# Attention in both directions and a maxout layer: exponentials without maxima, tested on chip, with a branch to a part that recomputes with maxima

## Chip, cores and metric

The kernel runs on one core of a Trainium2 chip. The metric is the device time of one execution in microseconds (us), as the median of several. The engines are named as in the profile: PE is TensorE's matmul, PEld its weight load, DVE is VectorE, ACT is ScalarE, POOL is GpSimd, SP is SyncE (it only issues transfers and waits). A name with a small q, as SPq, is an engine's queue of instructions that do no arithmetic: transfer issues, waits, drains.

## The reference

The inputs are `x` (8 batches, 8 heads, 512 rows, 64 columns) and `state` (8, 8, 32, 64), and four weight matrices. Per batch and head:

```python
scores = scale * x @ state.T                    # 512 x 32
a = exp(scores - scores.max(-1)); a /= a.sum(-1) + 1e-9
xread = a @ state                               # 512 x 64
scores2 = scale * state @ x.T                   # 32 x 512
a2 = exp(scores2 - scores2.max(-1)); a2 /= a2.sum(-1) + 1e-9
sread = a2 @ x                                  # 32 x 64
```

The 512 + 32 rows of the 8 heads side by side make 544 rows of 512 columns per batch, 4352 in all. Each goes through `h = max(X @ w1, X @ w2, X @ w3)` (512 to 768 columns) and `out = h @ w_out` (768 to 512). The inputs are normal numbers times 0.1.

## The kernel before

**Work per batch `b`.** `x_transpose` turns x (on PE, or by a transposing DMA on SP). `scores` multiplies it by the block-diagonal states `bd` and lets ACT take the exponential straight from the accumulators, into `e[b]`: the kernel subtracts no maximum, which changes nothing as long as the exponentials and their sums stay within the range of the numbers. `softmax` sums over the 32 states (line 183, DVE), takes reciprocals (185, DVE) and multiplies (186, POOL or DVE) into `a[b]`. `a_transpose` turns that. `sread` (line 207) uses the same `e` for the other direction: its matmul has columns of ones beside x, so that sums over the 512 rows come with the product; DVE takes the reciprocal of the sum (221, tile `rd`) and multiplies (223). A transposing DMA on SP, issued later, puts the result into `ats`.

**The maxout.** The reading `a @ state` is not formed: `g_cols` multiplies the states by slices of w1, w2, w3 (matmul in line 239, ACT copy in 245), and `x_maxout(b, m)` multiplies that by the transposed `a`, six matmuls of 512 columns for each of six slices `m` of 128 hidden columns. `s_maxout(m)` does the same for all state rows of the 8 batches at once, twelve matmuls of 256 columns. Both are `maxout` (line 253): matmuls in line 260 into three accumulators, ACT copies the first (264), DVE takes the maximum with the second (267) and with the third (268). `ffn_out` (line 280) does the last product, six matmuls (285) per 128 rows, an ACT copy (292) and an output DMA (296, 301). The very last call splits its copy between ACT (289) and DVE (290), and its output DMA is issued by SP.

**Order.** `tc.manual_schedule()` makes each engine issue its instructions in the order in which the text emits them; the framework adds the semaphores. The text staggers the batches: from `b = 2` on a loop runs `x_maxout(b, m)` for `m` in 0 to 5 and after each the functions in `slots[m]`: the next batch's scores, softmax, transposes and `g_cols`, and `ffn_out` of the batch before. For the last batch, `b = 7`, the slots hold `s_maxout(m)` and, in slots 1, 2, 4 and 5, one `ffn_out`. After the loop come six `ffn_out` calls: two of batch 7, two of the state rows, two of batch 7. The end (line 449 in the profile, where the framework's context closes) waits for all transfers, then brings the engines together.

**Buffers.** Accumulators: four one-bank buffers under the tag `pw`, taken in turn by nearly everything here, and two of two banks under `two`.

Of the kernel before, what the change touches and what calls it, by code (L numbers as in the profile page):

```python
# [8 lines left out]
F32 = mybir.dt.float32  # L9
BF16 = mybir.dt.bfloat16  # L10
AX = mybir.AxisListType
AF = mybir.ActivationFunctionType


@with_exitstack
def kernel(
# [14 lines left out]
    nc = tc.nc  # L31

    B, H, S, D = x.shape
    _, _, Ns, _ = state.shape
# [7 lines left out]
    J = 4  # L42
    HS = H // 2
    NM = d_ff // 128
    XW = H * J * D
    scale = 1.0 / (D ** 0.5)

    const = ctx.enter_context(tc.tile_pool(name="const", bufs=1))
    data = ctx.enter_context(tc.tile_pool(name="data", bufs=1))
    wpool = ctx.enter_context(tc.tile_pool(name="weights", bufs=1))  # L50
    work = ctx.enter_context(tc.tile_pool(name="work", bufs=2))
    pp = ctx.enter_context(tc.tile_pool(name="pp", bufs=2, space=bass.MemoryType.PSUM))
# [28 lines left out]
    ident = const.tile([128, 128], BF16, name="ident")  # L81
# [27 lines left out]
    warm = const.tile([128, 1], F32, name="warm")  # L109
    nc.scalar.activation(out=warm, in_=zero[:, 0:1], func=AF.Exp, scale=1.0)  # L110
    ats = data.tile([128, B, HS, Ns], BF16, name="ats")

    def keep_busy(n):
        p = pp.tile([128, 1024], F32, tag="two", name="idle")
        for _ in range(n):
            nc.tensor.matmul(p[:, 0:512], zero[:, 0:128], zero, start=True, stop=True)
# [21 lines left out]
    xT, e, a, aT, G, ht, osb = {}, {}, {}, {}, {}, {}, {}  # L138

    def new(d, b, shape, name, bufs=2):  # L140
        d[b] = work.tile(shape, BF16, tag=name, bufs=bufs, name=name)

    def x_transpose(b, g, copy):

        if g == 0:
            new(xT, b, [128, H, 2, 128], "xT")
        p = pp.tile([128, HS, 2, 128], BF16, tag="pw", bufs=4, name="pxt")
        for s in range(HS):
            for jj in range(2):
                nc.tensor.transpose(  # L150
                    p[:, s, jj, :],
                    xv[b][:, 2 * s + g, 2 * jj:2 * jj + 2, :].rearrange("p j d -> p (j d)"), ident)
        copy(out=xT[b].rearrange("p (s g) j t -> p g s j t", g=2)[:, g], in_=p)  # L153

    def x_transpose_dma(b):
        new(xT, b, [128, H, 2, 128], "xT")
        nc.sync.dma_start_transpose(out=xT[b].rearrange("p h j t -> p (h j) t"), in_=x_sb[b][:, 0:XW])

    def scores(b, g0, g1):
# [7 lines left out]
        for jj in range(2):  # L167
            for g in range(g0, g1):
                for s in range(HS):
# [5 lines left out]
                        stop=(g == g1 - 1 and s == HS - 1), skip_group_check=True)  # L175
        nc.scalar.activation(out=e[b][:, :, g0:g1], in_=p, func=AF.Exp, scale=scale)  # L176

    def softmax(b, g0, g1, mul):
        n = g1 - g0
        if g0 == 0:  # L180
            new(a, b, [128, J, 2, HS, Ns], "a")
        den = work.tile([128, J, n, HS], F32, tag=f"den{n}", name="den")
        nc.vector.reduce_sum(out=den, in_=e[b][:, :, g0:g1], axis=AX.X)  # L183
        rden = work.tile([128, J, n, HS], F32, tag=f"rden{n}", name="rden")
        nc.vector.reciprocal(out=rden, in_=den)  # L185
        mul(  # L186
            out=a[b][:, :, g0:g1].rearrange("p j g s n -> p j (g s) n"),
            in0=e[b][:, :, g0:g1].rearrange("p j g s n -> p j (g s) n"),
            in1=rden.rearrange("p j g s -> p j (g s)").unsqueeze(3).to_broadcast((128, J, n * HS, Ns)))
# [14 lines left out]

    late = []

    def sread(b):

        p = pp.tile([128, 2, 2, D], F32, tag="pw", bufs=4, name="psr")
        for j in range(J):  # L210
            for g in range(2):
                for s in range(HS):
                    xj = xv[b][:, 2 * s + g, j, :]
                    both = bass.AP(xj.tensor, xj.offset,
                                   (xj.ap[0], (XW - ((2 * s + g) * J + j) * D, 2), (1, D)))
                    nc.tensor.matmul(  # L216
                        p[32 * s:32 * s + 32, g], e[b][:, j, g, s, :], both,
                        start=(j == 0 and g == 0), stop=(j == J - 1), skip_group_check=True,
                        tile_position=(0, 32 * s))
        rd = work.tile([128, 2, 1], F32, tag="rd", name="rd")  # L220
        nc.vector.reciprocal(out=rd, in_=p[:, :, 1, 0:1])
        sr = work.tile([128, 2, D], BF16, tag="sr", bufs=B, name="sr")
        nc.vector.tensor_mul(out=sr, in0=p[:, :, 0, :], in1=rd.to_broadcast((128, 2, D)))
        late.append(lambda: nc.sync.dma_start_transpose(
            out=ats[:, b].rearrange("p s n -> p (s n)"), in_=sr.rearrange("p g d -> p (g d)")))
# [54 lines left out]
    def ffn_out(b, j, split=False):  # L280
        if j == 0:
            osb[b] = work.tile([128, J, d_model], F32, tag="osb", name="osb")
        p = pp.tile([128, d_model], F32, tag="pw", bufs=4, name="po")
        for m in range(NM):
            nc.tensor.matmul(p, ht[b][:, m, j * 128:(j + 1) * 128], wout_sb[:, m, :],  # L285
                             start=(m == 0), stop=(m == NM - 1))
        o = osb[b]
        if split:
            nc.scalar.copy(out=o[:, j, 0:256], in_=p[:, 0:256])
            nc.vector.tensor_copy(out=o[:, j, 256:512], in_=p[:, 256:512])  # L290
        else:
            nc.scalar.copy(out=o[:, j, :], in_=p)  # L292
        if b == "s":
            for k in range(4 * j, 4 * j + 4):
                r0 = k * SP + S
                (nc.sync if k % 4 < 2 else nc.gpsimd).dma_start(
                    out=out[r0:r0 + Ns, :], in_=o[32 * (k % 4):32 * (k % 4) + 32, j, :])
            return
        j0 = j if b == B - 1 and j >= 2 else j - 1
        if j == 1 or j == 3 or j0 == j:  # L300
            (nc.sync if b == B - 1 else nc.gpsimd).dma_start(  # L301
                out=out[b * SP:b * SP + S, :].rearrange("(p j) f -> p j f", j=J)[:, j0:j + 1, :],
                in_=o[:, j0:j + 1, :])


    def late_transposes():
        while late:
            late.pop(0)()

    dve, act, pool = nc.vector.tensor_copy, nc.scalar.copy, nc.gpsimd.tensor_copy  # L310
# [3 lines left out]
    states(0, act)  # L314
    for k in range(1, B // 2):
        nc.vector.memset(bds[k], 0.0)
    keep_busy(4)
    dve(out=x0_sb[0], in_=x0_f)
    x_transpose(0, 0, dve)
# [17 lines left out]
    for k in range(1, B // 2):  # L337
        load_st(k, nc.gpsimd)
    load_x(3)
    sread(0)  # L340
    g_cols(0, (1, 2))
    x_maxout(0, 1)
# [39 lines left out]
    for b in range(2, B):  # L382
        n = b + 1
        slots = [[] for _ in range(NM)]
        if n < B:
            if n == 3:
                slots[0].append(lambda: x_transpose(n, 0, act))
                slots[0].append(lambda: x_transpose(n, 1, dve))
                slots[3].append(lambda: x_transpose_dma(n + 1))
            elif n + 1 < B:  # L390
                slots[0].append(lambda: x_transpose_dma(n + 1))
            at = 1 if n == 3 else 0
            slots[at].append(lambda: scores(n, 0, 2))
            slots[at].append(lambda: softmax(n, 0, 2, nc.gpsimd.tensor_mul))
            slots[2 if n == 3 else 1].append(lambda: g_cols(n, (0, 1)))
            slots[2].append(lambda: a_transpose_dma(n))
            slots[3].append(lambda: sread(n))
            slots[4].append(lambda: g_cols(n, (2, 3)))
            slots[5].append(lambda: g_cols(n, (4, 5)))
            slots[4].append(late_transposes)  # L400
            if n % 2 and n + 1 < B:
                slots[3].append(lambda: states((n + 1) // 2, act))
            for k in ((4, 5) if n == 3 else (n + 2,)):
                if k < B:
                    slots[0].append(lambda k=k: load_x(k))
        else:
            for m in range(NM):
                slots[m].append(lambda m=m: s_maxout(m))
        for m in (1, 2, 3, 4, 5) if len(pending) > 4 else (1, 2, 4, 5):
            if pending:  # L410
                slots[m].append(lambda t=pending.pop(0): ffn_out(*t))
        for m in range(NM):
            x_maxout(b, m)
            for f in slots[m]:
                f()
        pending += [(b, j) for j in range(J)]
    assert pending == [(B - 1, j) for j in range(J)]
    ffn_out(B - 1, 0)
    ffn_out(B - 1, 1)
    ffn_out("s", 0)  # L420
    ffn_out("s", 1)
    ffn_out(B - 1, 2)
    ffn_out(B - 1, 3, split=True)


# [28 lines left out]
```

## Time and profile before

| | |
|---|---|
| runs, us | 166.25, 167.53, 166.08 |
| median of the runs, us | 166.25 |
| span of the profiled execution, first to last instruction, us | 164.5 |
| median minus that span, us | 1.75 |
| granted TensorE clock, share of full speed | 1.000 |
| DMA in all, MB | 20.94 |
| last PE matmul ends, us from the span's start | 160.3 |

For the profiled execution the profile gives the span alone; what lies around it is taken as the fourth row. In the profile's lists of groups, a line reads: line of the kernel, engine, operation, output <- input by the program's names, shapes, count, then busy time and mean ns of one, then idle time of the engine just before and what ended it. In the order of time, a line begins with start and duration in us. Lists of waits name who waited for whom, with total, number of times and the longest. The stages of the loop's last batch run from about 131.5 us to 151 us, and the six closing `ffn_out` calls from there to 160.3 us.

### The profile page before, as it was taken

To read this page: it belongs to the slowest core of one execution; us is meant where nothing else is said; L and a number is where in the kernel's file an instruction comes from. 1 tells how busy PE (TensorE), PEld (TensorE's weight loads), DVE (VectorE), ACT (ScalarE), POOL (GpSimd) and SP (SyncE) were. 2 spreads that over 40 slices of the span, in tenths; PEclk is the share of its full clock that TensorE was granted. 3 is DMA by queue.
4 is the path that set the end of the run, shared out by engine and by line. 5 is a ranking of instruction groups with operands and counts; after the bars stand their busy time and mean duration, and the time that the engine had idled before them with its cause. 6 is when DMAs were issued, how large, how long until landed. Compare 5 with 4: busy or idle time off the path is not lost.

```text
span 164.5 us, 3569 instructions
## 1 busy us (share of the span) xinstructions
PE 149.7 (91%) x1432; PEld 70.9 (43%) x1449; DVE 96.0 (58%) x162; ACT 99.1 (60%) x158; POOL 44.0 (27%) x64
## 2 busy tenths in 40 slices
PE   7658699988999999999999999999999999999990
PEld 2425243533445444434344434444444466665430
DVE  4675777889418553665548464865586455585001
ACT  3355578366896678853876688648755853333440
POOL 8975550106150601081016101410141010100140
PEclk9999999999999999999999999999999999999999
DMA  4999999800039999269992989460306030030373
GB/s 132 195 174 199 204 200 248 122 7 0 0 120 130 144 256 198 53 116 145 277 193 87 133 187 104 162 191 14 128 0 195 8 130 0 0 132 0 128 235 148
DMA packets 31824, 20.94 MB, mean 127 GB/s; under 512 B 17184, under 2 KB 29344, under 8 KB 31808
## 3 DMA queue, kind: packets, MB, share of 16 engines
q0 software_dynamic: 15632, 15.08, 46.3%
q1 hardware_dynamic: 16176, 5.64, 18.5%
q8 instruction: 11, 0.18, 0.5%
q14 instruction: 5, 0.04, 0.1%
HBM read 15.20 MB, written 8.91 MB: 147 GB/s over the span
## 4 chain that ended last, share of the span: by engine, by line
PE 63%; DVE 11%; ACT 10%; DMA 6%; POOL 4%; issue 4%; DVEq 0%; ACTq 0%; POOLq 0%
PE pw L260 34%; PE po L285 20%; DMA x<-in_x_dram 4%; PE pg L239 4%; DVE den L183 4%; DVE t L267 3%; ACT e L176 3%; ACT G L245 3%; DVE ht L268 3%; PE ps L171 2%; ACT t L264 2%; PE psr L216 2%; POOL w L94 1%; DMA out_dram<-osb 1%; POOL a L186 1%
## 5 line engine op out<-in xcount | busy, mean ns | idle before, releaser
L260 PE MATMUL pw<-aT,G 128*128 128x512 bf16 x288 | 71.2, 379 | 3.6 <-ACT G L245 1.8
L267 DVE TENSOR_TENSOR t<-t,pw 128x512 bf16<-128x512 bf16 (+1 forms) x54 | 35.1, 650 | 41.6 <-ACT t L264 40.0
L285 PE MATMUL po<-wout,ht 128*128 128x512 bf16 x188 | 47.9, 380 | 0.8
L260 PEld LDWEIGHTS <-G 128*128 128x128 bf16 x288 | 26.7, 98 | 36.2 <-issue 5.1
L245 ACT CAST G<-pg 128x768 bf16<-128x768 f32 x48 | 36.5, 805 | 8.0 <-PE pg L239 7.6
L264 ACT CAST t<-pw 128x512 bf16<-128x512 f32 (+1 forms) x54 | 30.5, 566 | 14.1 <-PE pw L260 12.6
L268 DVE TENSOR_TENSOR ht<-t,pw 128x512 bf16<-128x512 bf16 (+1 forms) x54 | 35.5, 658 | 5.6
L292 ACT COPY osb<-po 128x512 f32<-128x512 f32 x33 | 19.4, 587 | 21.2 <-PE po L285 20.7
L285 PEld LDWEIGHTS <-ht 128*128 128x128 bf16 x204 | 18.4, 98 | 23.6 <-issue 4.7
L301 POOL DMA_DIRECT2D out_dram<-osb x14 | 7.8, 559 | 70.2 <-ACT osb L292 70.2
L186 POOL TENSOR_TENSOR a<-e,rden 128x1024 bf16<-128x1024 bf16 (+1 forms) x8 | 14.4, 1800 | 33.4 <-DVE rden L185 19.8
L239 PE MATMUL pg<-w,bd 64*32 64x384 bf16 x384 | 13.0, 328 | 1.1 <-DMA w<-in_moe_w_dram 1.1
L183 DVE TENSOR_REDUCE den<-e 128x32 f32<-128x1024 bf16 (+1 forms) x9 | 9.9, 1095 | 2.6 <-ACT e L176 2.6
L176 ACT ACTIVATE e<-ps 128x1024 bf16<-128x1024 f32 x7 | 7.2, 1024 | 5.8 <-PE ps L171 5.8
L260 PE MATMUL pw<-ats,w 128*128 128x256 bf16 x72 | 8.8, 273 | 0.0
L239 PEld LDWEIGHTS <-bd 64*32 64x32 bf16 x384 | 3.6, 89 | 11.7 <-issue 11.7
L260 PEld LDWEIGHTS <-w 128*128 128x128 bf16 x72 | 7.0, 98 | 2.1
L94 POOL DMA_DIRECT2D w<-in_moe_w_dram x9 | 6.8, 770 | 0.0
L69 POOL DMA_DIRECT2D x<-in_x_dram x7 | 6.7, 957 | 0.0
L150 PE MATMUL pxt<-ident,x 128*128 128x128 bf16 x64 | 4.4, 219 | 2.2 <-DMA x<-in_x_dram 1.1
L134 ACT COPY bd<-pt 64x512 bf16<-64x512 bf16 x6 | 3.5, 580 | 4.2 <-PE pt L131 4.1
L171 PEld LDWEIGHTS <-xT 128*128 128x128 bf16 x128 | 4.7, 98 | 2.4 <-DVE xT L153 0.8
(42 smaller groups left out, 63.4 us busy)
## 6 DMA issues: line engine op xcount, KB each, us to landing
out_dram<-osb POOLq DMA_DIRECT2D x14, 512.0 KB, 3.7
x<-in_x_dram POOLq DMA_DIRECT2D x7, 512.0 KB, 9.0
w<-in_moe_w_dram POOLq DMA_DIRECT2D x3, 384.0 KB, 10.3
w<-in_moe_w_dram POOLq DMA_DIRECT2D x3, 256.0 KB, 8.2
wout<-in_moe_w_out_dram POOLq DMA_DIRECT2D x1, 768.0 KB, 16.4
x0f<-in_x_dram SPq DMA_DIRECT2D x1, 512.0 KB, 4.0
out_dram<-osb SPq DMA_DIRECT2D x1, 512.0 KB, 2.7
out_dram<-osb SPq DMA_DIRECT2D x2, 256.0 KB, 2.2
```

Source lines behind the costliest of these rows:

```text
L94: nc.gpsimd.dma_start(out=w_sb[c][:, :, i, :], in_=w.rearrange("(kk p) f -> p kk f", p=128)[:, :, m0 * 128:m1 * 128])
L176: nc.scalar.activation(out=e[b][:, :, g0:g1], in_=p, func=AF.Exp, scale=scale)
L183: nc.vector.reduce_sum(out=den, in_=e[b][:, :, g0:g1], axis=AX.X)
L186: mul(out=a[b][:, :, g0:g1].rearrange("p j g s n -> p j (g s) n"), in0=e[b][:, :, g0:g1].rearrange("p j g s n -> p j (g s) n"), in1=rden.r ...
L239: nc.tensor.matmul(p[32 * s:32 * s + 32, g, 0:384].rearrange("p (i f) -> p i f", i=3), bd(b, 2 * s + g)[64 * g:64 * g + 64, g, :], w[64 * ...
L245: copy(out=G[b][:, :, m * 384:(m + 1) * 384], in_=p[:, :, 0:384])
L260: nc.tensor.matmul(p[:, 0:n], lhs(i, k), rhs(k), start=(k == 0), stop=(k == nk - 1))
L264: nc.scalar.copy(out=t0[:, 0:n], in_=pw[0][:, 0:n])
L267: nc.vector.tensor_max(t1[:, 0:n], t0[:, 0:n], pw[1][:, 0:n])
L268: nc.vector.tensor_max(ht[b][:, m, :], t1[:, 0:n], pw[2][:, 0:n])
L285: nc.tensor.matmul(p, ht[b][:, m, j * 128:(j + 1) * 128], wout_sb[:, m, :], start=(m == 0), stop=(m == NM - 1))
L292: nc.scalar.copy(out=o[:, j, :], in_=p)
```

## The change

1. The sums of `softmax` and the reciprocals of `sread` are no longer kept in rotating work tiles but in one tile `seen`, 34 numbers per batch and partition.
2. `check_range`, in slot 1 of the last batch and ahead of `s_maxout(1)`, takes the largest and smallest of all 272 numbers of each partition, compares them with 1e18 and 1e-18, sums the 128 x 2 verdicts over the partitions by a matmul with ones, and sets `flag` to 1 unless all are good.
3. At the end, behind the last `ffn_out`, every engine loads `flag` into a register and branches: where it is 0, over a part that does everything again with maxima subtracted (`x_transpose` to `ffn_out` for all 8 batches, one after the other). With these inputs the part is not executed.
4. `mark_branch_hint_location`, ahead of the six closing `ffn_out` calls, puts an instruction into every engine's queue that names the branch labelled `again` as likely taken.

The core of the diff:

```diff
+    seen = data.tile([128, B, J * H + 2], F32, name="seen")
...
-        den = work.tile([128, J, n, HS], F32, tag=f"den{n}", name="den")
+        den = seen[:, b, 0:J * H].rearrange("p (j g s) -> p j g s", j=J, g=2)[:, :, g0:g1]
...
-        rd = work.tile([128, 2, 1], F32, tag="rd", name="rd")
+        rd = seen[:, b, J * H:J * H + 2].unsqueeze(2)
...
+    flag = data.tile([128, 1], I32, name="flag")
+    ones = const.tile([128, 128], BF16, name="ones")
+
+    def check_range():
+        v = seen.rearrange("p b k -> p (b k)")
+        top = work.tile([128, 2], F32, tag="top", name="top")
+        nc.vector.tensor_reduce(out=top[:, 0:1], in_=v, op=ALU.max, axis=AX.X)
+        nc.vector.tensor_reduce(out=top[:, 1:2], in_=v, op=ALU.min, axis=AX.X)
+        ok = work.tile([128, 2], BF16, tag="ok", name="ok")
+        nc.vector.tensor_scalar(out=ok[:, 0:1], in0=top[:, 0:1], scalar1=1e18, scalar2=None, op0=ALU.is_le)
+        nc.vector.tensor_scalar(out=ok[:, 1:2], in0=top[:, 1:2], scalar1=1e-18, scalar2=None, op0=ALU.is_ge)
+        p = pp.tile([128, 2], F32, tag="pw", bufs=4, name="pst")
+        nc.tensor.matmul(p, ones, ok, start=True, stop=True)
+        n = work.tile([128, 1], F32, tag="nok", name="nok")
+        nc.vector.reduce_sum(out=n, in_=p, axis=AX.X)
+        nc.vector.tensor_scalar(out=flag, in0=n, scalar1=255.5, scalar2=None, op0=ALU.is_le)
...
     for k in range(1, B // 2):
         nc.vector.memset(bds[k], 0.0)
+    nc.gpsimd.memset(ones, 1.0)
     keep_busy(4)
...
         else:
+            slots[1].append(check_range)
             for m in range(NM):
                 slots[m].append(lambda m=m: s_maxout(m))
...
+    tc.mark_branch_hint_location("again", "LikelyTaken", list(mybir.ALL_ENGINES))
     ffn_out(B - 1, 0)
     ffn_out(B - 1, 1)
     ffn_out("s", 0)
     ffn_out("s", 1)
     ffn_out(B - 1, 2)
     ffn_out(B - 1, 3, split=True)
...
+    bad = nc.values_load(flag[0:1, 0:1], min_val=0, max_val=1)
+    with tc.If(bad != 0, label="again"):
+        for b in range(B):
+            x_transpose(b, 0, act)
+            x_transpose(b, 1, dve)
+            scores_below_max(b)
+            softmax(b, 0, 2, nc.vector.tensor_mul)
+            a_transpose(b, 0, act)
+            a_transpose(b, 1, dve)
+            sread_below_max(b)
+            late_transposes()
+            for m in range(NM):
+                g_cols(b, (m,))
+            for m in range(NM):
+                x_maxout(b, m)
+            for j in range(J):
+                ffn_out(b, j)
+        for m in range(NM):
+            s_maxout(m)
+        ffn_out("s", 0)
+        ffn_out("s", 1)
```

`scores_below_max` and `sread_below_max` are new and stand in the skipped part alone; they take the maxima from the accumulators on DVE and subtract them ahead of the exponential.

## The prediction

> **What bounds the kernel now.** I read the page's busy shares first, then the chain of work that ended last, then the busy time by stages around the two places that the change touches, and last the order of time inside those places.
>
> ```profile
> span 164.5 us, 3569 instructions
> PE 149.7 (91%) x1432; PEld 70.9 (43%) x1449; DVE 96.0 (58%) x162; ACT 99.1 (60%) x158; POOL 44.0 (27%) x64
> ...
> PE 63%; DVE 11%; ACT 10%; DMA 6%; POOL 4%; issue 4%; DVEq 0%; ACTq 0%; POOLq 0%
> ```
>
> TensorE (PE) is busy for 91% of the span and holds 63% of the chain. An average hides the stage, so here is the busy time of each engine (PE, weight loads, DVE, ACT, POOL, with counts), the granted clock and the DMA share for the last 34 us:
>
> ```profile
> 130.00:135.40 5.40, 5.40 (x46) 2.96 (x31) 3.21 (x7) 3.54 (x6) 0.53 (x1) 1.00 0.25 99
> 135.40:150.00 14.60, 14.49 (x92) 9.06 (x93) 8.76 (x17) 5.30 (x11) 0.53 (x1) 1.00 0.10 37
> 150.00:160.30 10.30, 10.21 (x52) 4.94 (x51) 1.86 (x4) 3.89 (x8) 2.54 (x5) 1.00 0.42 143
> 160.30:164.50 4.20, 0.00 (x0) 0.00 (x0) 0.42 (x1) 0.37 (x1) 0.00 (x0) 1.00 0.40 149
> ```
>
> From 130 to 160.3 PE idles 0.2 us in 30, at full clock. Any wait put into PE's queue there moves the end by its whole length: nothing later has idle time that could take it back. From 160.3 to 164.5 PE does nothing; that stretch is the last copies, the last output transfer and the closing barrier.
>
> **The change, part by part.**
>
> *Sums kept in one tile, and the ones.* Sums and reciprocals go to `seen`, with the same operations, sizes and engine (DVE). Price 0: all writers and readers of the tile are DVE. `ones` adds one POOL fill of 128x128 bf16; the same fill for the identity took 0.2 us. POOL sat idle 0.95 us ahead of its first multiplication at 9.56 us, waiting for DVE, and the fill stands ahead of that multiplication: 0. Without this cover it would cost its 0.2.
>
> *The test in slot 1 of the last block.* This is the dear part. The text puts `check_range` behind `x_maxout(7, 1)` and ahead of `s_maxout(1)`, and each engine issues in the order of the text. In order of time, first PE's instructions there and then DVE's (start, duration):
>
> ```profile
> 134.12 1.46 PE L260 MATMUL pw<-aT,G 128*128 128x512 bf16 x6
> 135.41 1.47 PE L260 MATMUL pw<-ats,w 128*128 128x256 bf16 x12
> ```
>
> ```profile
> 135.37 0.69 DVE L267 TENSOR_TENSOR t<-t,pw 128x512 bf16<-128x512 bf16 x1 [0.21 <-ACT t L264]
> 136.16 0.69 DVE L268 TENSOR_TENSOR ht<-t,pw 128x512 bf16<-128x512 bf16 x1
> 136.77 0.41 DVE L267 TENSOR_TENSOR t<-t,pw 128x256 bf16<-128x256 bf16 x1
> ```
>
> Six matmuls of `x_maxout(7, 1)`, then twelve of `s_maxout(1)`; the DVE pair of 512 columns belongs to the former. The reader is to see the lag: PE goes on to `s_maxout(1)` at 135.41, while DVE is busy with the maxima of the products before it until 136.85 and takes its next work at 136.77 (starts overlap ends a little). The new matmul on `ones` and `ok` stands in PE's queue at 135.41 and needs DVE's verdict, so PE waits, and behind it all that is left of PE's work: five `s_maxout`, four `x_maxout` and the remaining `ffn_out`. ACT and DVE wait for those in turn; SP has its output transfers behind them, POOL too.
>
> How long? DVE first does two reductions over 8 x 34 = 272 numbers, then two comparisons on one column.
>
> ```profile
> L183 DVE TENSOR_REDUCE den<-e 128x32 f32<-128x1024 bf16 x7 | 8.5, 1220 | 2.1 <-ACT e L176 2.1
> ...
> L183 DVE TENSOR_REDUCE den<-e 128x16 f32<-128x512 bf16 x2 | 1.3, 658 | 0.5 <-ACT e L176 0.5
> ...
> L221 DVE RECIPROCAL rd<-psr 128x2 f32<-128x2 f32 x8 | 1.3, 157 | 0.0
> ```
>
> Reductions: 658 ns for 512 and 1220 for 1024 give 1.10 ns an element and 96 ns at rest, so 0.395 us for 272. Max and min instead of sum, float32 instead of bf16, are not in this trace. Twice the rate would make 0.25 each; I take the row's rate. Comparisons: the smallest DVE row is the reciprocal on 2 columns, 0.16. So the verdict is ready at 136.77 + 2 x 0.395 + 2 x 0.16 = 137.88. From DVE to PE takes 0.06 (the cast of x ends at 5.89, the weight load that waited for it starts at 5.95), and the matmul itself about 0.1 before the next can start (weight loads of 98 ns stand in every PE row here). `s_maxout(1)` then starts at 138.0 instead of 135.41: **+2.6 us**. Below: reductions of 0.25 and comparisons of 0.11 (the fastest reciprocal): 2.2. Above: 0.1 between dependent DVE instructions (136.06 to 136.16 above) and 0.2 more on PE: 3.1. The two DVE instructions behind the matmul, sum and flag, some 0.3 us, delay DVE when it has caught up: `s_maxout(1)` has only just begun. They cost 0. The extra accumulator buffer is freed by the first of them, long before its turn comes again.
>
> *The branch.* At the end each engine loads the flag into a register, compares, and jumps over the part that recomputes everything. The trace of before shows no register load and no jump. First what covers them, in the order of time, in SP's waits, and in the closing line's own instructions:
>
> ```profile
> 159.61 1.89 SPq L301 DMA_DIRECT2D out_dram<-osb  x2
> ```
>
> ```profile
> SPq L449 <- DMA out_dram<-osb: 1.6, 2, 1.2
> ```
>
> ```profile
> L449 SPq EVENT_SEMAPHORE  x7: 28/28/28, 163.2 to 163.6; - x7
> ```
>
> ```profile
> L449 PEldq DRAIN  x1: 4075/4075/4075, 156.2 to 156.2; - x1
> L449 POOLq DRAIN  x1: 4021/4021/4021, 159.0 to 159.0; - x1
> ```
>
> SP issues the last transfer by 161.50 and then waits 1.6 us in all for landings, until 163.2. It clears seven semaphore waits 0.06 us apart until 163.6, and the barrier follows. So SP has 1.6 us in which a load and a jump are free. PE's queue is at the end at 156.2 and only drains, 4 us ahead: free as well. ACT and DVE finish at 160.7 and 161.1 with about 2.5 us to spare before the barrier at 163.7. The hint is one more instruction in each queue (0.06), in front of PE's last 8 us and ahead of waiting queues elsewhere: 0. POOL's closing drain runs from 159.0 to 163.0.
>
> A register load lies between a semaphore instruction (0.06 us a step) and a small transfer from issue to landing (128 KB by SP: 2.1). It fetches like the one, but a single word, and it runs in the queue like the other; near neither, it gets the middle, 1.0. A compare and jump is one more step of the queue, 0.1. The path that skips has to leave the semaphores as the other path would; I allow eight steps, 0.5 (from 0 to sixteen, 1.0, for as many transfer semaphores). Together 1.6 for each engine. On SP this just fits in its 1.6. On POOL it comes before the drain: if the drain ends with the transfers, nothing is lost; if its 4.0 us start anew at 159.6 + 1.6 (its last issue ends at 159.6), it ends at 165.2, 1.5 after the 163.7 at which the barrier stands now. I take the middle, **+0.7**, with 0 and 2.6 as ends (drain anew, load at 2.1).
>
> [...] The trace shows instruction fetches only as transfers (queue, packets, MB, share of the transfer engines' time):
>
> ```profile
> q8 instruction: 11, 0.18, 0.5%
> q14 instruction: 5, 0.04, 0.1%
> ```
>
> Eleven of 16 KB (one per 260 PE instructions) in 0.5% of the time of 16 transfer engines, 16 x 164.5 us, make 1.2 us each; five of 8 KB in 0.1% make 0.5. With 2.1 for a round trip, a jump that has to fetch costs 3.3 on PE and 2.6 elsewhere. If the hints, which stand six `ffn_out` calls ahead of the branch, do their work, this is paid beside them, and I take 0. If they don't: DVE jumps at 160.7 + 1.0 + 0.1, is back at 164.4, and at the barrier at 164.9 instead of 163.7: 1.2, or 2.3 with the longer load. [...]
>
> [...]
>
> **Sum.** The profiled execution's span is 164.5; the median of the runs is 166.25, 1.75 above it, for what lies around the span, and I keep that. 164.5 + 2.6 + 0.7 = 167.8; + 1.75 = **169.6**, 2.0% slower.
>
> **The rivals.**
>
> *Hints without effect.* For: a recomputing part of some 200 instructions on DVE and ACT and thousands on PE puts the target beyond the next fetch. Against: the hint stands on every engine, and PE is 4 us ahead anyway. 166.25 + 2.6 + 1.2 to 2.3 = 170.1 to 171.2, and up to 171.8 if SP has to fetch as well (its jump would be back 2.6 us later, its own 1.6 are used up).
>
> *A branch that stops everything.* If the engines must finish all transfers before they load the flag, load, jump and matching semaphores (1.6) come after 163.6, and a fetch of 2.6 may join: 166.25 + 2.6 + 1.6 to 4.2 = 170.5 to 173.1. For: a part with its own transfers must be entered with known semaphore counts. Against: each engine can carry its own waits, as L449 does now.
>
> *The test off PE's path: not slower.* If DVE took the four test instructions ahead of slot 1's maxima (it is idle for 0.21 us before 135.37), the verdict would be there at 135.19 + 1.11 = 136.3, and PE would wait 1.05; the maxima then free their accumulators 1.1 later, which costs the third product group some 0.4. With the branch covered: 166.25 + 1.5 = 167.75. It decides from a total below 1.66 on. Against: the order of the text holds on DVE too.
>
> **How the numbers follow.** A measurement here tells about 1% from no change: 167.9 and 164.6 are the borders. Chances: my forecast 0.64 (its own range 168.4, with 2.2 and 0, to 170.9, with 3.1 and 1.5), hints without effect 0.17, everything stopped 0.11, off PE's path 0.07; 0.01 for something that gains. The range leaves out the not-slower case and the upper half of the stopped one, and takes in both upper ends of the forecast, 3.1 + 2.6: 168.4 to 172.0. Faster 0.01, same 0.08, slower 0.91.
>
> **What would show it.** Right: a PE idle of about 2.5 us ahead of `pst` near 135.4, ended by DVE; two DVE reductions of about 0.4; no PE idle after it; the last PE matmul at 162.9 instead of 160.3; the stretch from there to the end 4.2 to 5.7 long. Wrong: PE idle under 1.6 at the test (the lag was read wrongly); reductions far from 0.4; an end stretch of over 6 us, with an engine waiting behind its jump (hints), or with all loads after 163.6 plus the shift (everything stopped).

## The result and the profile after

The changed kernel took 171.98 us (median of 4 runs, 170.44 to 172.85) against 166.58 us for the kernel before (median of 4): ratio 1.031 (1.024 to 1.039), 3.1% slower. The forecast was 169.6 us with a range to 172.0. The direction and both costly places were forecast; the sum was 2.4 us short. Of all the runs in this document a few took over 1.5% longer than the fastest of their kernel; the ratios leave these out, the medians do not.

The page of the kernel after, its busy shares and its two queues of instruction fetches:

```profile
span 168.6 us, 3614 instructions
...
PE 150.8 (89%) x1433; PEld 71.4 (42%) x1450; DVE 97.2 (58%) x168; ACT 99.1 (59%) x158; POOL 44.1 (26%) x65
...
q8 instruction: 12, 0.20, 0.5%
q14 instruction: 7, 0.06, 0.1%
```

PE's busy time is 1.1 us longer than before and the span 4.1: what was added is mostly waiting. There are three instruction fetches more in all (one on q8, two on q14, 0.04 MB together), so by far the most of the skipped part's thousands of instructions are not fetched.

Three stretches hold what matters, and every run below is read by them. A runs from the first matmul of `s_maxout(0)` to the first of `s_maxout(1)`, B from there to the end of PE's last matmul, C from there to the end of the span (us, one profiled execution each):

| kernel | A | B | C |
|---|---|---|---|
| before | 2.60 | 24.84 | 4.21 |
| after | 5.00 | 24.84 | 6.64 |
| after, profiled again | 5.00 | 26.53 | 6.38 |

A grows by 2.40 and C by 2.43. The two profiles of the same changed kernel differ by 1.69 in B, where nothing was changed. (The profiled execution of after reached `s_maxout(0)` 0.65 us earlier than that of before, a difference in its start, so its span grew by 2.40 + 2.43 - 0.65 = 4.18.)

Stretch A, the kernel after in order of time:

```profile
135.52 0.69 DVE L271 TENSOR_TENSOR ht<-t,pw 128x512 bf16<-128x512 bf16 x1
136.12 0.43 DVE L318 TENSOR_REDUCE top<-seen 128x1 f32<-128x272 f32 x1
136.47 0.43 DVE L319 TENSOR_REDUCE top<-seen 128x1 f32<-128x272 f32 x1
136.81 0.15 DVE L321 TENSOR_SCALAR ok<-top 128x1 bf16<-128x1 f32 x1
136.93 0.15 DVE L322 TENSOR_SCALAR ok<-top 128x1 bf16<-128x1 f32 x1
137.14 0.16 PE L324 MATMUL pst<-ok,ones 128*128 128x2 bf16 x1 [2.20 <-DVE ok L322]
```

PE was idle for 2.20 us ahead of `pst`, until the last comparison: the forecast's order of events, with starts 0.35 apart for the reductions, not their full 0.43.

The busy time by stages, the kernel after (two stages of 3.41 us around the wait, then B, then C; columns as in the prediction):

```profile
132.86:136.27 3.41, 2.07 (x14) 1.14 (x12) 2.89 (x7) 0.90 (x2) 0.00 (x0) 1.00 0.38 154
136.27:139.68 3.41, 2.49 (x18) 1.78 (x19) 1.97 (x8) 0.37 (x1) 0.00 (x0) 1.00 0.00 0
137.16:162.00 24.84, 24.68 (x142) 13.98 (x144) 9.67 (x20) 9.19 (x18) 3.07 (x6) 1.00 0.23 82
162.00:168.60 6.60, 0.00 (x1) 0.00 (x0) 0.42 (x1) 0.37 (x1) 0.00 (x0) 0.88 0.28 99
```

Behind the wait PE is busy 24.68 of 24.84 us at full clock. Nothing is given back, and here nothing more is lost.

Stretch C. The jump and the semaphore steps of the path that skips (line of the `If`; duration in ns least/median/most, then first and last start):

```profile
L497 SPq EVENT_SEMAPHORE  x8: 17/17/17, 164.8 to 166.0; - x8
L497 POOLq EVENT_SEMAPHORE  x4: 17/43/43, 162.9 to 163.5; - x4
...
L497 POOLq COMPARE_BRANCH  x1: 59/59/59, 161.5 to 161.5; - x1
...
L497 ACTq COMPARE_BRANCH  x1: 68/68/68, 162.6 to 162.6; - x1
L497 ACTq EVENT_SEMAPHORE  x1: 17/17/17, 163.0 to 163.0; - x1
...
L497 POOLq INC_SWDGE_SEM  x1: 958/958/958, 163.6 to 163.6; - x1
...
L497 SPq COMPARE_BRANCH  x1: 64/64/64, 164.2 to 164.2; - x1
```

and the closing line, us 163 to 168 of the kernel after:

```profile
L542 POOLq DRAIN  x1: 3243/3243/3243, 164.6 to 164.6; - x1
```

POOL's chain ends last. It jumps at 161.5, steps four semaphores that wait for landings (162.9 to 163.5; its last output, issued at 160.8, lands 2.6 us later), runs one `INC_SWDGE_SEM` (0.96) and only then begins its drain, 3.24 us, until 167.8; the barrier follows. In the kernel before, the drain began at 159.0 and was over at 163.0, ahead of SP. SP is second here: jump at 164.2, eight steps of its own, done at 166.9.

### The profile page after: what moved, and what is told of

It is laid out like the page before. It is cut to its first block, busy times and chain, and to the rows that moved or that the text cites. A ratio compares the mean times of both kernels' runs of the same rounds, so it can differ in the third digit from the quotient of the medians.

```text
span 168.6 us, 3614 instructions
## 1 busy us (share of the span) xinstructions
PE 150.8 (89%) x1433; PEld 71.4 (42%) x1450; DVE 97.2 (58%) x168; ACT 99.1 (59%) x158; POOL 44.1 (26%) x65
## 3 DMA queue, kind: packets, MB, share of 16 engines
q1 hardware_dynamic: 16176, 5.64, 14.9%
## 4 chain that ended last, share of the span: by engine, by line
PE 63%; DVE 12%; ACT 10%; DMA 4%; POOL 4%; issue 4%; DVEq 0%; POOLq 0%; ACTq 0%
PE pw L263 33%; PE po L288 22%; DMA x<-in_x_dram 4%; PE pg L242 4%; DVE seen L186 4%; DVE t L270 4%; DVE ht L271 3%; ACT e L179 3%; ACT G L248 3%; ACT t L267 2%; PE ps L174 2%; PE psr L219 2%; POOL w L96 1%; POOL a L189 1%; ACT osb L295 1%
## 5 line engine op out<-in xcount | busy, mean ns | idle before, releaser
L186 DVE TENSOR_REDUCE seen<-e 128x32 f32<-128x1024 bf16 (+1 forms) x9 | 9.9, 1095 | 2.6 <-ACT e L179 2.6
L119 PE MATMUL idle<-zero 128*128 128x512 bf16 x12 | 5.2, 569 | 1.3 <-DVE zero L82 1.3
```

## The experiments

Each run's stretches, its median and its ratio to the kernel before on the same chip (95% interval):

| run | A | B | C | us | ratio |
|---|---|---|---|---|---|
| e1_test_alone | 5.00 | 26.41 | 4.21 | 169.9 | 1.024 (1.017 to 1.031) |
| e2_branch_alone | 2.61 | 24.84 | 6.70 | 168.8 | 1.015 (1.007 to 1.022) |
| e3_no_hints | 5.00 | 26.53 | 6.74 | 172.8 | 1.040 (1.032 to 1.048) |
| e4_verdict_later | 2.60 | 25.15 | 6.38 | 169.8 | 1.022 (1.011 to 1.034) |
| after_again | 5.00 | 26.53 | 6.38 | 172.4 | 1.032 (1.026 to 1.038) |
| e7_pe_kept_busy | 5.01 | 24.84 | 6.55 | 171.4 | 1.028 (1.023 to 1.032) |
| e5_no_pool_end | 5.00 | 26.52 | 7.15 | 172.9 | 1.033 (1.026 to 1.040) |
| e6_three_moved | 2.61 | 25.15 | 6.30 | 168.7 | 1.015 (1.010 to 1.020) |
| e8_skipped_by_sp | 5.00 | 26.45 | 5.64 | 171.4 | 1.030 (1.025 to 1.036) |
| e9_best | 2.60 | 25.15 | 6.01 | 169.5 | 1.019 (1.013 to 1.025) |
| e10_test_later_alone | 2.60 | 25.15 | 4.21 | 166.9 | 1.003 (0.999 to 1.006) |
| e11_small_part | 2.61 | 25.15 | 4.25 | 167.0 | 1.004 (1.001 to 1.007) |

### The test alone, and the branch alone

`e1_test_alone` keeps the test and has no hint, no load, no branch and no recomputing part:

```diff
-    tc.mark_branch_hint_location("again", "LikelyTaken", list(mybir.ALL_ENGINES))
...
-    bad = nc.values_load(flag[0:1, 0:1], min_val=0, max_val=1)
-    with tc.If(bad != 0, label="again"):
-        ...
```

> The test of the sums without the register loads, the branch, the hints and the skipped part (the flag is written and not read). My account after reading the trace of the changed kernel: the test costs one PE wait of 2.4 us and the end is as before, so about 2.4 us over the kernel before, 169.0 against 166.6, with the last PE matmul 4.2 us ahead of the end of the span. Rival: the pause also lowers the granted clock for the rest, then 1 us or more on top, 170 or later. Rival: the test is cheap and all of the loss is at the branch, then 166.6 to 167.5.

`e2_branch_alone` keeps the branch and leaves out the test; the flag is a constant 0:

```diff
-    nc.gpsimd.memset(ones, 1.0)
+    nc.vector.memset(flag, 0)
...
-            slots[1].append(check_range)
```

> The loads, the branch, the hints and the skipped part without the test: the flag is set to 0 once near the start, the ones are left out too. My account: the stretch from PE's last matmul to the end grows from 4.2 to 6.6 us because POOL's closing drain starts 3 us later, behind its jump and its semaphore steps, and takes over 3 us again; so about 2.4 us over the kernel before, 169.0. Rival (jump fetches): the same size of loss, but the last engine at the closing barrier is one that waits behind its jump and not POOL's drain. Rival (clock): loss above 3.5, with granted clocks below those of the kernel before.

The branch alone cost 2.4 us by its ratio, and C is 2.5 longer. The test alone cost 3.9, although A grew by 2.40 only. The other 1.6 is in B. The test alone, by stages:

```profile
133.30:136.70 3.40, 1.36 (x7) 0.49 (x6) 2.98 (x9) 0.58 (x1) 0.00 (x0) 1.00 0.22 89
136.70:140.10 3.40, 3.23 (x15) 2.09 (x15) 1.27 (x5) 0.37 (x1) 0.00 (x0) 0.50 0.00 0
140.10:163.30 23.20, 23.20 (x131) 12.64 (x129) 8.51 (x16) 8.81 (x17) 3.06 (x6) 1.00 0.24 87
```

The reader is to see the column that stands third from the right, the granted clock: 0.50 in the 3.40 us after the wait, and 1.00 on both sides. Half a clock for 3.4 us is worth, as an estimate, half of 3.4, 1.7 us, beside the 1.6 in B. In the kernel after, profiled again, the same:

```profile
135.58:138.99 3.41, 1.20 (x12) 0.95 (x11) 2.51 (x8) 0.37 (x1) 0.00 (x0) 1.00 0.00 0
138.99:142.40 3.41, 3.41 (x12) 1.43 (x10) 0.84 (x2) 0.06 (x1) 0.00 (x0) 0.50 0.00 0
```

The difference from the first profile of after is where the wait falls. There it lay across the edge at 136.27 (that profile's clock falls to 0.50 at 166.99, nine times 3.41 us later, when PE's work is over), and PE was busy 2.07 and 2.49 us of the two periods: full clock. Here it fell into one period, with 1.20 busy (1.36 in the test alone): half clock in the next. This is a new term, found by the run that was to confirm the wait, and `e7` tests it.

### The wait, and the clock behind it

`e4_verdict_later` takes the product with ones, its sum and the flag out of `check_range` and puts them into slot 3, two slots later:

```diff
+        verdict.append(ok)
+
+    verdict = []
+
+    def sum_verdict():
+        ok = verdict.pop()
         p = pp.tile([128, 2], F32, tag="pw", bufs=4, name="pst")
...
             slots[1].append(check_range)
+            slots[3].append(sum_verdict)
```

> The changed kernel with the matmul that sums the verdicts, and the two DVE instructions behind it, moved from slot 1 to slot 3 of the last block; the two reductions and comparisons stay in slot 1. My account: PE's wait of 2.4 us goes to nearly nothing, since the verdict is then ready some 5 us before PE comes to the matmul; DVE's 1.2 us fit in its idle time; about 2.4 us under the changed kernel, 169.6 if that one is at 172.0. Rival: the reductions delay the maxima of s_maxout(1) and PE waits for accumulators instead, then a gain of less than 1.2 us.

PE in order of time, the verdict two slots later:

```profile
141.90 1.46 PE L263 MATMUL pw<-aT,G 128*128 128x512 bf16 x6
143.19 0.17 PE L330 MATMUL pst<-ok,ones 128*128 128x2 bf16 x1
143.22 1.75 PE L263 MATMUL pw<-ats,w 128*128 128x256 bf16 x12
```

No idle time stands beside `pst` any more, A is back at 2.60, and no half clock appears. B is 0.31 longer, which the extra matmul brings where it now stands: the twelve `s_maxout` matmuls behind it took 1.75 us instead of 1.47. (Its four times, 168.7 to 171.4, scatter more than the stretches explain; the shortest two, of which the profiled one is one, fit A, B and C: 166.0 + 0.3 + 2.2 = 168.5.)

`e7_pe_kept_busy` leaves the wait and fills it with matmuls on a tile of zeros, the kernel's own warm-up helper:

```diff
+        keep_busy(11)
         p = pp.tile([128, 2], F32, tag="pw", bufs=4, name="pst")
```

> The changed kernel with eleven matmuls on zeros (512 columns each) put ahead of the verdict's matmul, so that PE works on nothing useful instead of waiting, for about the same 2.4 us. If the wait as such is all of the cost, the time equals that of the changed kernel. If the idle PE lowers its clock for 3.41 us (up to 1.7 us of matmul time), the time falls by 1.0 to 1.7 us and the granted clock in the runs stays at 0.99 or more, although the same time passes until s_maxout(1) starts.

PE in order of time, kept busy:

```profile
137.91 2.54 PE L119 MATMUL idle<-zero 128*128 128x512 bf16 x11
140.29 0.17 PE L325 MATMUL pst<-ok,ones 128*128 128x2 bf16 x1
140.32 1.47 PE L263 MATMUL pw<-ats,w 128*128 128x256 bf16 x12
```

and by stages, the wait and what follows it:

```profile
136.90:140.30 3.40, 3.40 (x18) 1.51 (x17) 2.91 (x8) 0.59 (x1) 0.00 (x0) 1.00 0.17 69
140.30:165.20 24.90, 24.86 (x146) 14.01 (x144) 9.67 (x20) 9.20 (x19) 3.07 (x6) 1.00 0.23 82
```

Useful work waits as long as in after (A 5.01), but PE is busy meanwhile, the clock stays at 1.00, and B is 24.84 instead of the 26.53 of `after_again`, which ran beside it:

> The changed kernel once more, as the partner of the next three on the same chip. Account: PE wait 2.4 us + longer end 2.4 us + a stretch of half clock behind the wait (seen in the trace of the test alone: 3.41 us at 0.50 from 136.7 on) in the runs in which the wait falls into one clock period; so 4.8 to 6.5 us over the kernel before, the lower granted clocks (0.985 and less) with the longer times.

One profile of `e7` would not decide it, since the first profile of after kept its clock as well, with PE idle. All 14 profiles of these kernels together do: while PE still had work ahead, seven periods of 3.41 us held 1.2 to 1.45 us of PE work, and each was followed by a period at half clock; none with 1.48 us (`e3_no_hints`, from 162.63 us) or more was. Five of the seven lie at this wait. So idleness, not the late verdict, halves the clock. The times lean the same way, 171.4 against 172.4, but their intervals overlap. The other two half-clock periods are in the start-up (`e7` at 13.3 us, `e2` at 14.15), ahead of A, B and C; such periods are a likely reason why the granted clocks of the runs of `e7` did not stay at 0.99, as had been expected, but went down to 0.976.

A gap of 2.2 us was enough when it fell into one period (1.20 us of PE work in `after_again`), and was not when two shared it (2.07 and 2.49 in the first profile of after).

`e10_test_later_alone` is `e4` without hint, load, branch and recomputing part:

```diff
+            slots[3].append(sum_verdict)
...
-    tc.mark_branch_hint_location("again", "LikelyTaken", list(mybir.ALL_ENGINES))
...
-    bad = nc.values_load(flag[0:1, 0:1], min_val=0, max_val=1)
-    with tc.If(bad != 0, label="again"):
-        ...
```

> The test alone, with its matmul in slot 3, without loads, branch, hints and skipped part. Account: all of the test's cost was PE's wait and the clock behind it, so this is the kernel before within 0.5 us (0.3 us of it at the matmul in slot 3). Rival (the DVE work or the sums kept in one tile cost by themselves): 1 us or more over the kernel before.

Its ratio, 1.003 (0.999 to 1.006), can't be told from no change; the profile shows the 0.31 us in B that `e4` has too. Where PE does not wait for it, the test costs no more than that.

### The hints

`e3_no_hints`:

```diff
-    tc.mark_branch_hint_location("again", "LikelyTaken", list(mybir.ALL_ENGINES))
```

> The changed kernel without the five hint instructions, which the trace shows at 0.7 us from the start of the span and not ahead of the closing output products. If hints so early do nothing, the time stays that of the changed kernel (172.0 median, span 168.6 in the profiled run) within 1 us. If they are what keeps the jumps short, ACT, DVE, SP or POOL show 2 us or more between their compare-and-branch and their next instruction instead of about 0.5, and the time grows by 1 to 2.6 us.

The line of the `If`, without hints:

```profile
L496 SPq EVENT_SEMAPHORE  x8: 17/17/17, 168.2 to 169.2; - x8
...
L496 PEldq COMPARE_BRANCH  x1: 3520/3520/3520, 160.9 to 160.9; - x1
...
L496 ACTq COMPARE_BRANCH  x1: 50/50/50, 164.8 to 164.8; - x1
...
L496 DVEq COMPARE_BRANCH  x1: 72/72/72, 165.5 to 165.5; - x1
L496 SPq COMPARE_BRANCH  x1: 45/45/45, 166.3 to 166.3; - x1
L496 ACTq EVENT_SEMAPHORE  x1: 17/17/17, 168.3 to 168.3; - x1
L496 DVEq EVENT_SEMAPHORE  x1: 21/21/21, 169.1 to 169.1; - x1
```

From the jump to the next instruction ACT takes 3.5 us (164.8 to 168.3), DVE 3.6, and PE's jump itself lasts 3.52. SP takes 1.9 (166.3 to 168.2). With hints ACT took 0.4 (162.6 to 163.0), DVE 0.6 (163.3 to 163.9), SP some 0.5, and PE's jump lasted 0.39. POOL's next step waits for a landing in both kernels, so it can't be read from POOL. So the hints work: they save some 3 us on PE, ACT and DVE and 1.3 on SP. The time did not grow by the 1 us or more expected with that: C moves only from 6.38 or 6.64 to 6.74. PE, ACT and DVE are not the last to arrive, and POOL's drain, over at 169.6, covers most of what SP loses; SP, ready at 170.0, is the last here. That such a jump has to fetch was the author's estimate (3.3 us on PE, 2.6 elsewhere); this run shows a wait, with 3.5 us, and four instruction fetches more than after, not that the wait is for them.

### What makes the end longer

`e5_no_pool_end` gives POOL no transfers from the hint on: the closing outputs and those of the skipped part go by SP.

```diff
-                (nc.sync if k % 4 < 2 else nc.gpsimd).dma_start(
+                (nc.sync if k % 4 < 2 else outq[0]).dma_start(
...
+    outq = [nc.gpsimd]
...
     tc.mark_branch_hint_location("again", "LikelyTaken", list(mybir.ALL_ENGINES))
+    outq[0] = nc.sync
```

> The changed kernel with no transfers issued by POOL in the six closing output products nor in the skipped part; SP issues them. Account (POOL's drain is what ends last): POOL's drain then starts before 158 and is done long before the end, its step of nearly 1 us for software transfers is gone, and the closing barrier waits for SP, at 166.9 in the trace of the changed kernel instead of 167.8: 0.9 us faster. SP issues four more transfers of about 0.4 us and steps more semaphores, which can take some of it back. Rival (a jump or the fetch is last): no gain.

A miss: C is 7.15. POOL's drain now begins at 157.6 and is out of the way, but SP issues the closing outputs one after the other:

```profile
160.50 4.39 SPq L299 DMA_DIRECT2D out_dram<-osb  x8
164.99 1.22 SPq L304 DMA_DIRECT2D out_dram<-osb  x2
```

Eight smaller issues instead of four stand ahead of the last two, so the last issue began 1.8 us behind the end of PE's last matmul instead of 0.9, and SP's landing and steps followed.

`e6_three_moved` is `e4`, the above, and the load moved ahead of the six closing `ffn_out`:

```diff
+            slots[3].append(sum_verdict)
...
+    outq[0] = nc.sync
+    bad = nc.values_load(flag[0:1, 0:1], min_val=0, max_val=1)
     ffn_out(B - 1, 0)
...
-    bad = nc.values_load(flag[0:1, 0:1], min_val=0, max_val=1)
```

> Three edits in the changed kernel: the verdict's matmul in slot 3, no POOL transfers at the end or in the skipped part, and the register loads of all engines ahead of the six closing output products instead of behind them. Account: the test is free (no PE wait, no half clock), POOL is out of the end, and SP saves its load and range check of 0.9 us; what stays is the jump and 6 to 9 semaphore steps of SP behind the last transfer, so 0.8 to 1.8 us over the kernel before, 167.0 to 168.0 where that is at 166.2. If the loads put ahead cost PE or ACT time in their queues, or the end is bound by something else than SP's steps, 169 or more.

It missed as well (C 6.30, 2.5 us over before), by the same queue of issues on SP.

`e8_skipped_by_sp` therefore, with `outq` as in `e5`, leaves the closing outputs on POOL and moves only the skipped part's to SP:

```diff
     bad = nc.values_load(flag[0:1, 0:1], min_val=0, max_val=1)
+    outq[0] = nc.sync
```

> The changed kernel with the output transfers of the skipped part issued by SP instead of POOL; the four of POOL in the closing products stay. Account: POOL then has no semaphore steps and no step for software transfers behind its jump, so its drain of some 3.4 us starts 3 us earlier and ends ahead of SP; the barrier waits for SP at about 4.9 us behind PE's last matmul and the stretch from there to the end falls from 6.4 to 6.7 us to 5.7. Rival (the drain has to wait for landings or is not what ends last): the stretch stays at 6.4 or more.

C fell to 5.64. The closing line of this kernel:

```profile
L545 POOLq DRAIN  x3: 40/103/3250, 164.2 to 169.9; - x3
L545 SPq DRAIN  x3: 7/7/13, 169.3 to 169.6; - x3
```

POOL's drain begins at 164.2, takes 3.25 and ends at 167.5; SP is ready at 169.3 and sets the end. So of the 2.4 in C, 1.0 came from POOL's chain being later than SP's (6.64 - 5.64, or 0.7 from 6.38), and the other 1.4 is SP's own: the last landing some 0.6 later than in before (2.6 instead of 2.0 from its issue), and 0.8 for the longer row of steps behind that landing.

`e9_best` joins `e4`, `e8` and the early load:

```diff
+            slots[3].append(sum_verdict)
...
+    bad = nc.values_load(flag[0:1, 0:1], min_val=0, max_val=1)
     ffn_out(B - 1, 0)
...
-    bad = nc.values_load(flag[0:1, 0:1], min_val=0, max_val=1)
+    outq[0] = nc.sync
     with tc.If(bad != 0, label="again"):
```

> Three edits in the changed kernel: the verdict's matmul in slot 3, the skipped part's transfers on SP with POOL's four closing ones kept, and the register loads ahead of the six closing output products. Account: no PE wait (0.3 us lost at the matmul in slot 3), no half clock behind it, SP free of its load and range check and of the four extra issues that delayed the last transfer by 1 us when it had all eight; the stretch behind PE's last matmul comes to 4.8 to 5.3 us against 4.2 before, so 0.9 to 1.4 us over the kernel before. Rival (SP's semaphore steps and the late landing of the last transfer set the end whatever else is moved): 6 us or more of stretch, 2 us or more over the kernel before.

A miss, and the rival's numbers: C was 6.01, no gain from the early load, though SP reaches its steps at 163.5. It then waits there for the last landing, which comes 2.9 us after its issue. Load and jump were covered already.

`e11_small_part` is `e4` with a skipped part of one instruction. The part that recomputes is left out:

```diff
     with tc.If(bad != 0, label="again"):
-        for b in range(B):
-            ...
+        nc.vector.memset(flag, 0)
```

> The kernel with the verdict's matmul in slot 3, all loads, hints and branches kept, but with a single fill on DVE as the part that is jumped over: what recomputes everything is left out (with these inputs it isn't executed either way). Account: the branch's cost is not the load and the jump but what a large part with its own transfers brings to the path that skips it (semaphore steps on SP and POOL behind the landings, POOL's drain later, fetches of instructions behind the jump among the last output's packets). Then the stretch behind PE's last matmul falls from 6.4 us to 4.3 to 5.0, with the last output landing 2.0 us after its issue on all queues again and POOL's drain of some 3.5 us ending near SP's last step, and the time is 0.4 to 1.1 us over the kernel before. Rival (load and jump themselves, 0.9 us on SP and some 0.7 elsewhere, are the cost): the stretch stays at 5.5 or more.

C is 4.25, as in before, with load, comparison, jump and hints in place. Its closing line:

```profile
L531 SPq EVENT_SEMAPHORE  x14: 17/28/28, 162.5 to 164.2; - x14
L531 POOLq EVENT_SEMAPHORE  x4: 17/17/17, 163.5 to 164.2; - x4
L531 POOLq DRAIN  x3: 40/103/3250, 159.7 to 164.0; - x3
```

POOL's drain starts at 159.7, 0.2 behind its jump, with no step between, and is over by 163.0, before SP. So a load and a jump cost nothing at this end; what costs comes with the large part. `e11` takes away its transfers and its size at once. That POOL's share comes from the steps for the part's transfers is shown by `e8`; SP's longer row of steps is read from the traces (8 at the `If` and 14 in the closing line in after, the 14 alone in `e11`).

One thing stays open, why transfers land later. The transfers of the last stretch, kernel after:

```profile
q14 instruction: 3, 0.02, 1.9%
...
out_dram<-osb SPq DMA_DIRECT2D x1, 256.0 KB, 2.7
```

and with the small part:

```profile
out_dram<-osb SPq DMA_DIRECT2D x1, 256.0 KB, 2.0
```

Three instruction fetches fall behind the jumps in after, `e8` and `e9` (landings after 2.7, 2.6 and 2.9 us); none in before, `e10` and the small part (2.0 each). Without hints, in `e3`, there are six, and the last landing comes 3.7 us after its issue. It is not the last transfer alone. The eight 64 KB outputs ahead of it, before and then after:

```profile
out_dram<-osb SPq DMA_DIRECT2D x4, 64.0 KB, 2.1
out_dram<-osb POOLq DMA_DIRECT2D x4, 64.0 KB, 2.3
```

```profile
out_dram<-osb SPq DMA_DIRECT2D x4, 64.0 KB, 3.3
out_dram<-osb POOLq DMA_DIRECT2D x4, 64.0 KB, 3.1
```

SP's four take 3.0 to 3.3 us in all eight profiles with the large part in which POOL issues its four, and 2.1 in the four without the part (before, `e1`, `e10`, `e11`). POOL's steps behind the jump start right behind POOL's own of these landings. While they are under way, behind PE's jump at 158.8, one 16 KB fetch on q8 falls in after and none in before. Later landings and fetches go together in all these runs; a run that has the one without the other was not made, so the cause is not shown. No version tried is faster than the kernel before.

## Why the prediction was right and wrong

- **Sums in one tile, ones: 0.** Held: B is 24.84 in after and before, and `e10` as a whole can't be told from before.
- **The wait: 2.6.** Measured 2.40, inside 2.2 to 3.1. The reductions took 0.43 each, but started 0.35 apart; the comparisons 0.15. The lag was read rightly.
- **"Nothing later has idle time that could take it back."** Held. But the clock was taken as 1.00 throughout, and that failed: when the wait falls into one period of 3.41 us, PE runs the next at half clock, 1.6 to 1.7 us. This is in neither the sum nor a rival. It is in `e1`, `e3`, `e5`, `e8` and `after_again`, and not in the first profile of after. Of the other three runs of after, whose granted clocks are 0.976 to 0.985 against its 0.995, it can be inferred, not shown: a half-clock period in the start-up, as in `e2` and `e7`, lowers them too.
- **The branch: +0.7 as the middle of 0 and 2.6.** Mis-sized: 2.43 in after (2.17 in `after_again`), near the upper end. The step that failed is "if the drain ends with the transfers, nothing is lost": the drain takes 3.24 us even from a start 3.3 us behind POOL's last issue (3.25 in `e8` and `e11`), and it starts 3.0 us behind the jump because four steps wait for landings and 0.96 goes to `INC_SWDGE_SEM`. Averaging the two mechanisms gave a number that neither of them produces.
- **SP's 1.6 us of cover.** Load (0.55) and jump (0.5) did fit under the landing; in `e11` C is 4.25. But the eight semaphore steps were counted among what fits, and all but the first (at 164.8) stand behind the landing, not beside it.
- **Register load 1.0, jump 0.1.** Measured 0.47 to 0.81 and 0.4 to 0.5 to the next instruction with hints.
- **Rivals.** *Hints without effect* fell: they work, and without them C would be longer by 0.1 to 0.4 (`e3`), not by 1.2 to 2.3. That a jump has to fetch is shown by no run; `e3` shows that without hints PE's jump lasts 3.52 us and that ACT and DVE take 3.5 and 3.6 to their next instruction, SP 1.9. *Everything stopped* fell: SP loads the flag at 163.3, while its last transfer is still on its way. Its argument, known semaphore counts, does return behind the jump, as SP's eight steps and POOL's four. By the total alone, 171.98, this rival (170.5 to 173.1) would have been picked before the forecast; the order of events decides against it. The upper end of the hints, 171.8, does not follow from the terms given, 166.25 + 2.6 + 2.6 = 171.45. *The test off PE's path* fell, as DVE's order of time in A shows.
- **The sum.** 166.3 + 2.4 + 2.4 = 171.1 without the half clock, 172.8 with it. The four runs lie between 170.4 and 172.9. The forecast's 169.6 lacks 1.7 of the branch and, in such runs, 1.7 of the clock, and has 0.2 too much for the wait. That the median stands inside the range, by 0.02 us, is partly luck: two of the four runs lie above 172.0. The upper end was two terms at their dearest, a wait of 3.1 and a branch of 2.6; the wait was cheaper, and a clock that the sum did not have filled the gap. One of the forecast's own signs of being wrong appeared too, an end of over 6 us (6.64), but with POOL's drain as the last and not with either of the causes named there.

## What to carry to other kernels

A test on chip costs next to nothing (0.3 us here) if the busiest engine asks for its verdict well after it is ready; ask at once and it pays the whole chain (2.4 us here), and perhaps a period at half clock behind that (1.6 to 1.7 us). Price a branch by what the path that skips must do after the last landing, above all on an engine with a long closing drain (POOL's 3.24 us here), not by the load and the jump (with them and the small part C was 4.25, before 4.21). Where one cost hangs on which of two mechanisms holds, take the one that the engine's order makes likelier and keep the other as a rival; their mean is a forecast of neither.

## What the runs showed of the hardware

- An idle gap of 2.2 us ahead of one matmul halved the granted clock for the next 3.41 us when PE was busy only 1.20 (`after_again`) to 1.36 us (`e1`) of one 3.41 us period; with 2.07 and 2.49 busy in two periods (after) it did not. Over all 14 profiles, while PE still had work ahead, the seven periods followed by half clock held 1.2 to 1.45 us of PE work, and none with 1.48 (`e3`) or more was followed by one.
- POOL's closing drain behind its software transfers took 3.24 to 3.25 us from its own start, whether it follows the jump at once (`e11`, at 159.7) or the steps behind the landings (after, at 164.6). It took 3.63 in `e5`, 3.92 in `e9` and 4.02 in before, so 3.24 is the least seen, not a constant.
- The jump over the large part took 0.4 us to ACT's next instruction with a hint (after) and 3.5 without (`e3`); on SP it was 0.5 and 1.9. The hints were issued at 0.7 to 0.8 us of the span, not where the text has them, and worked all the same:

```profile
L542 POOLq BRANCH_PREFETCH_HINT  x1: 51/51/51, 0.7 to 0.7; - x1
...
L542 DVEq BRANCH_PREFETCH_HINT  x1: 51/51/51, 0.8 to 0.8; - x1
```
